# Another replay order for a hand-scheduled attention and MLP kernel: 1449 operations in a new sequence, 113 of them on another engine

## The chip, the core and the metric

The kernel runs on one core of a Trainium2 chip. A core has a matrix engine (TensorE, PE in the profile), a vector engine (VectorE, DVE), an activation engine (ScalarE, ACT), a general engine (GpSimd, POOL) and a sequencer that only issues transfers (SyncE, SP). Each engine takes its instructions strictly in the order in which the program lists them, and the engines meet through semaphores. The metric is the device time of one execution in microseconds (us); the figure of a kernel is the median of several runs.

## The reference

Two stages follow one another: a linear attention with cosine and sine weights, and a two-layer MLP with the gate `h * cos(h)`.

```python
# q, k, v: (8, 8, 576, 64) float32
r = maximum(x, 0); phi(x) = concat([r * cos(theta), r * sin(theta)], -1)   # theta by position
kv  = einsum('bhsf,bhsd->bhfd', phi(k), v);  z = sum(phi(k), axis=2)
num = einsum('bhsf,bhfd->bhsd', phi(q), kv); den = einsum('bhsf,bhf->bhs', phi(q), z) + 1e-6
x   = (num / den) as (4608, 512)
h   = x @ w_in                       # w_in (512, 2048)
out = (h * cos(h)) @ w_out           # w_out (2048, 512), out (4608, 512) float32
```

## The kernel before

The work is cut by batch. For a batch b of the eight, the attention loads q, k and v through SP, makes the features (`feat`, lines 240 and 242: a ReLU times a cosine or sine column, ten pieces of 128x512 for q and ten for k), casts v (`val`, line 222), multiplies k features with v on PE (`kv_half`, line 278), copies the result out (`kvz`), transposes the q features, multiplies them with kvz (`num_half`, line 287), divides (`den_add` and `ratio`, lines 295 to 307) and transposes the quotient into `xT`. For batches 0 and 1 the transposes of q and x, and for batch 2 those of x, run on PE (line 337); the later ones are DMA transposes that SP issues (lines 343 and 736). Four token tiles of a batch are one group of the MLP; the fifth tiles of all batches form one more group, `r`. The groups go in the order 0 to 6, `r`, 7.

The MLP's first layer (`moe1`, line 353, and `quad`, line 414 for groups 6, `r` and 7) multiplies xT with w_in into one of four PSUM slots called `m1`; ACT takes the cosine of it (`sin`, line 420), DVE or sometimes POOL multiplies both (`gate`, line 366) into `g`, and the gate frees the slot. The second layer (`prod`, line 469) uses a Strassen-Winograd form with seven products instead of eight for 2x2 blocks; it needs sums of blocks of g (`sums`, written to `s` and `g`), of w_out (`weight_sum`, WT), of w_in (`w_in_sum`, WS) and of x (`x_sum`, xs), all of them through line 366 on DVE or POOL. `z_add` and `y_add` of that form are DVE operations between a product and the next product into the same PSUM bank.

Nothing of the order is left to a scheduler. The functions `attention`, `layer1`, `quads` and `layer2` only register operations in a list, each with its number, the engines that could run it and its dependencies. `Plan.run` then walks through a text of 1449 entries, `ORDER`, and emits the operations in just that sequence:

```python
for x in ORDER.split():
    name, _, ids = x.partition(":")
    o, ids = self.ops[int(name.rstrip("VAG"))], [int(i) for i in ids.split(",") if i]
```

An entry such as `546:1` is operation 546 with buffer slot 1 of the ring it takes from; a letter behind the number picks the engine where there is a choice: V is DVE, A is ACT, G is POOL. Operations without a letter are PE's matmul groups, SP's and POOL's DMA issues, or bookkeeping. Since every engine runs its own instructions in this order, an entry that waits holds back all later entries of its engine, and a PE entry that waits holds back all of PE. The slot numbers matter too: `m1` has 4 slots, `qp`, `qT` 4, `ch` 3, `kvz` 3, `g` 2, and a slot's new user waits for its last one.

Entries that the text below speaks of, by number:

- 29, 30, 27: k features of batch 0 (DVE, DVE, ACT). 63 and 65: the two halves of its k-v product. 58, 60: transposes of its q tiles 3 and 4. 13 and 62: matmuls on zeros ("dummy").
- 247, 249: transposes of q tiles 2 and 3 of batch 1. 164, 160: first-layer tiles 6 and 5 of group 0, second half; 147, 159, 163, 167: the gates of tiles 1, 4, 5, 6. 213, 216, 228: features of batch 1. 253, 255: its k-v products; 254: the copy of the first one. 257: its first numerator.
- 303 to 312: the sums of w_out. 319, 320: the late sums of group 0. 360, 367, 369: k features of batch 2. 395: its k-v product.
- 422, 424, 427, 429, 432, 434: loads of q, k, v of batch 3 (two each). 393: DMA transpose of q tile 4 of batch 2. 437, 439, 441, 445, 446: k features of batch 3; 457, 461: two casts of its v; 969: a store of group 1; 472: the k-v product of batch 3. 443, 910, 919: a k feature of batch 3 and two gates of group 2.
- 488, 493: DMA transposes of x tiles 2 and 3 of batch 3. 546: DMA transpose of q tile 1 of batch 4. 492: the quotient that 493 reads; 532: a q feature that 546 reads. 983: the first matmul group on xT of batch 3.
- 1306, 1358: a gate of group 6, a `z_add` of group `r`. 1463, 1465, 1474, 1475: two `x_sum` and a `z_add` of group 7, and the matmul group that needs 1474.

Of the kernel before, what the change touches and what calls it, by code (L numbers as in the profile page):

```python
# [54 lines left out]
14 172:0 176:1 884:2 17:0 107:0 819:1 16:0 183:1 182:1 343:2 13 32V:0 34V:1 33A 35V 36A:2 52:0  # L55
54:1 53V:0 37A 38V:3 55A:1 56:2 40V:0 4G 24V 28A 5G 25V 62:3 31A 23V 7G 44A 30V 9G 39A 22V 41V
57A:2 42G 26V 45G 58:0 48V 51G 43A 60:1 46V 49G 27A 47V 29V 11G 61A:0 50V 63:0 59V:3 65:1 64V
66A 180 67:0 68V 77:1 69V:0 78A 72:0 79V:1 70:3 73A 71A 74V 87:1 80:2 88A 81A 89V:2 82:0 112:1
83A 84V 90:0 97:1 91V 102:0 98A 85:3 103A 108:2 99V:1 86A 184 75:0 76A 100:3 104V 92:1 93A 113
186 101A 94V 116:0 114A:0 189 109 115V 120:3 110A:1 191 117 111V 194 121 118A:2 136:1 122A:0  # L60
119V 95:2 196 137 96A 123V 128:0 138A:1 199 129 139V 124:2 130A:2 201 132:3 131V 133 105:1
134A:0 125 106V 148:0 126A:1 135V 144:1 223A:1 127V 149 140:3 150A:2 224G 225V:2 152:2 227V:3
226A 153 151V 141 154A:0 145 228V 142A:1 243:0 204G 155V 214A 205G 143V 245:2 244A:0 207G 215V
156:3 221V 146A:2 160:0 209G 213V 161 218A 147V 157 211G 220A 233V 164:1 237G 229V:0 158A:0 165
219G 216V 239A 159V 217A 230V 247:3 222A 235V 240G 231A:1 238V 234V 236V 246A:1 232G 173V 248A:3
253:2 174V 302V 166A:1 345 313:0 304V 254A 347 241A 167V 303G 242A 350 162A:2 257:3 255:2 352
258V 259V:0 249:1 256A 341 163V 262:3 250A:2 272:2 305G 321:1 263V 273V 264V 267:0 277:1 268V
265:3 278A 269V:2 266A 355 314 274V 306G 270:3 279V:1 315A:0 275:0 282:2 271A 316 357 276A 283A
280:1 284V 317 308G 281V 285:3 318A 287:0 286V 292:2 168:1 288V 293A 289V:2 260:3 370A:2 324:0
261V 294V 371A 307G 290:0 888:0 251:3 291V 372A:3 385:0 295:2 252V:1 169 296A 824:0 344:0 170A:0  # L70
825 820:3 826A:1 171V 374G:0 848:2 361A 827V 836:1 297 366A 319V 832:0 420:1 502:0 373A 175V
362G 821 833 822A:2 387:1 177V 849 834A:0 837 823V 850A:1 325 835V 380G 381A 856:3 309V 382G
384A 844:0 178V 375G 326A:1 845 857 846A:2 851V 322 838A:0 847V 852:2 383A 941:1 839V 179G 389:3
828:0 298A 364A 853 323V 840:1 854A:1 327V 829 365A 841 299V:1 328 320G 830A:2 855V 842A:0 331
368A 831V 300:2 329 301A 843V 360G 376A:1 310V 868:0 864:2 378A:2 332 330V 377A 367G 860:1 311V
858A:1 391:2 336 333A 861 859V 363A 337 334G 312V 862A:2 949:0 892:0 338A 369G 379V 865 863V 422
869 866A:0 880:3 424 870A:1 867V 881 339G 427 872:1 871V 882A:2 876:2 429 883V 877 393:1 873
885V 878A:0 395 421:1 874A:1 879V 396 875V 959:0 397A 418 889V 398 950 399A 886V 400V:0 960
951A:1 447A:3 957 890V 432 961A:2 449G:0 887V 952 945:2 891V 403 401:3 404A 958 405V:2 402A 434
448G 450A 953 1025:0 962V 451A:1 406:2 955V 408 452A 963 407V 462:0 439G 446A 409V 966 410V:1  # L80
453A:2 464:1 964 956V 954A 437G 454A 411:1 965V 413 967 412A 414V 415V:0 466:3 438A 971 441G
968V 416:3 468:2 457A 972 417V 460A 440V 917:2 976:1 443V 458A 969G 973V 455A:3 893:1 442V
918A:2 461G 920:0 444V 894A:0 919V 445G 899:3 921A:1 895V 456A 923:2 922V 900A:2 470:0 896:1
974G 924A:0 901V 459A 905:0 504 925V 897A:1 506 472 906A:2 898V 509 908:3 907V 511 473 909A:0
935:2 474A 500 910V 514 475 936A:1 929:1 476V 477V:2 926:0 930A:2 937V 478 480 927A:0 931V 911:3
481A 928V 902:2 912A:1 516 482V:1 914:1 903A:2 529G:0 913V 932:0 915A:0 483 904V 1033:0 933A:1
916V 530G 531A:1 934V 1034 533A:2 942V 485 938:3 1035A:1 486V 487V:0 532G 544:0 524A 1036 503:0
939A:2 943V 490 488 534A 491V 1041 940V 521G 528A 492V:2 546:1 1037 520A 525V 1038A 495 493 946V
579:1 661:2 542A 541G 1043:0 496A 947V 535G:3 540A 548:3 1044 1029:1 948V 539A 1042 519A 1040V
523A 1109:2 543G 527V 983:2 944V 536A 998:1 1039V 537A:0 550:2 986:0 497V:1 522A 538G 526A 995:3  # L90
1045V:0 498 999A:0 554 1046V 996A:1 552:0 555 1000V 984A:2 1047 577 997V 556A 581 985V 987A:0
557 992:1 583 558A 988V 586 1001:3 993A:1 559V:0 588 977:2 1002A:2 994V 560 562 978A:0 1003V
989:0 563A 979V 591 980:1 990A:1 564V:2 1010:3 981A:2 991V 567 593 1011A:0 1013:2 982V 606A:1
568V 1026G 1004:0 569V:1 1014A:1 565 1048 1005A:2 1012V 607A 572 1049V 570 1007:1 608G:2 573A
1006V 1050 1008A:0 1027V 621:0 596A 1051 1028V 602A 609G 1019:3 610V:3 1052A 574V:0 1055 1020A:2
612A:0 575 1021V 1016:0 1053G 1009V 613A 1117:0 623:1 1015V 617G 1017A:2 1056 620A 600V 611G
601V 616A 1118 1060:0 1057V 603A 1022:3 1018V 604A 619G 625:3 614V:1 1073:1 580:1 1023A:0 605G
1119A:1 1024V 1079:2 627:2 1074A:1 1030V 1120 597A 1075V 1058G 1082:0 618A 1031V 599A 1067:3
598G 1032V 1083A:2 1076:1 1068A:0 1084V 615A 1121 1069V 1077A:1 629:1 1064:0 1124V 1122A 1078V
1123G 1061:3 1065A:2 663 1080A:0 1066V 1125 665 1062A:1 1081V 668 1070:1 1063V 670 631 1071A:2  # L100
673 632 1072V 1127:0 633A 659 1110V 675 634 1113:0 1111V 1094:0 635A 636V:2 1126 1095A:0 637
1096V 639 1085:2 640A 688G:2 641V:1 1128 1086A:1 1112V 642 644 1129A:1 1193:1 1100:3 1087V
690G:3 689A 1130V 1088:1 645A 703:0 1101A:2 646V:0 1131 685A 680G 1102V 684A 649 1132 678V 683A
691V 1103:0 647 681A 1133V 679G 1097:2 1104A:0 687V 705:1 650V 1089A:1 1105V 1139 699A 1090V
1091:3 1098A:2 692G:0 651V:2 700A 1134 698A 1099V 652 654 702A 1135 738:1 694G:1 693V 1092A:0
707:3 1140 1136V 682A 1093V 701A 1201:0 1144:1 1137G 696A:2 1141V 1160:0 695V 697A 1142G 1154:1
709:2 1161A:1 1202 1155A:2 1162V 686G 740 655A 1156V 1151:2 1203A:1 742 656V:1 1148:3 1152A:0
1153V 1145:0 657 1149A:1 1150V 1157:1 1146A:2 711:1 1147V 1106:2 1158A:0 1159V 1204 1107A:1
662:0 1108V 713 745 1114V 1205 747 1115V 714 1206A 750 1209 1116V 715A 736 752 765A:3 1208V 716
1210 767V:0 1163:3 769V:1 768A 1207V 770G 771A:2 1211:0 766V 1164A:2 717V 1212 1197:2 780:0  # L110
718V:0 772A 1169:0 1310:0 1213A:2 1165V 719 1166:1 1170A:0 1214V 755G 757A 1171V 721 1172:2
782:1 1167A:1 722V 723V:2 756A 1178:3 763G 1173A:2 760V 1215 724 1168V 759A 726 1174V 1184:0
727A 784:3 776A 1194G 728V:1 1179A:0 1175:1 1185A:1 1180V 729 1181:2 1176A:2 1186V 731 1182A:0
775G 1216 786:2 1195V 777A 779G 1183V 1218 773A:3 1196G 1177V 764A 1219 732V 733V:0 762A 1187:3
1220A 1217V 734 1190:0 778G 1188A:1 758V 1221G 761A 1318:0 739:1 1189V 1191A:0 1223 1242V 774A
790 788:0 1192V 1319 1229V 1224 1230V 1232V 1233:2 1225A 1228:0 1198V 1234:1 1320A:1 1226G 791
1236V:0 1235A:3 1321 1231G 792A 1238 1253:0 1239A:2 1199G 1326 1240V 1237 793 1241V 1322 794A
795V:2 1200G 1243 1323A 1247 1244V 796 798 1248A:1 1254:2 799V 1245A:0 1250 1249V 1327 1251A:2
1324G 800V:1 1255A:1 1328:0 1252V 1256A:1 801 1257 1314:1 1258 1261V 1246G 1329 1259A:1 1260V
1262 1330A:2 1426:2 1325G 1266 1263V 803 1267A:2 1272:3 1331V 804A 1269 1264A:0 1268V 1332  # L120
1270A:1 805V:0 1265G 1273:0 1333 1275A:0 1271V 806 1311G 1274A:2 808 1334V 1335 809A 810V:2 1277
1276 1278A:2 811 813 1280V 1312G 1291:1 814A 815V:1 1281 1285 1282V 1336 816 1286A:0 1287V
1283A:1 1288 1340 1337A 1284G 1279V 1289A:0 1292:0 1290V 1434:0 1338G 1293A:3 1313V 1294A:1 1296
1295 1297A:2 1341 1299V 1298V 1300 1342A 1345:1 818 1301V 1343G 1435 1302A:1 1307 1436V:1 1304
1308A:0 1346G 1350:2 1305A:2 1309V 1437 1348G 1306V 1351:1 1438 1353A:2 1347V 1352A:3 1303V 1442
1439A 1440V 1369:0 1355 1349V 1354 1315G 1356A:0 1370 1358V 1444:0 1371A 1357V 1372A:0 1359
1430:0 1388:2 1360V 1373 1316V 1361A:2 1366 1363 1367A:1 1441V 1443 1364A:0 1368V 1362G 1445
# [925 lines left out]
```

## Time and profile before

| what | value |
|---|---|
| runs | 300.44, 298.2, 298.97, 299.27, 299.67 us |
| median | 299.27 us |
| the profiled execution, its own time | 300.44 us |
| its span, first to last instruction | 298.7 us |
| mean granted TensorE clock | 0.979 |
| PE matmul busy | 278.0 us (93%) |
| DVE busy | 239.8 us (80%) |
| ACT busy | 196.8 us (66%) |
| POOL busy | 187.9 us (63%) |

The profiled execution is the slowest of the five: its own time is 1.17 us above the median, and 1.74 us of it lie outside the span. Busy is the time in which the engine had an instruction under way; matmuls overlap, so a busy PE is not a PE at its full rate. An idle stretch in brackets in the timeline is the time the engine stood still before an instruction, with what released it.

### The profile page before, as it was taken

Reading aid. Unit: us, or ns where it says so; the run is one execution under the profiler, and the core shown is the slowest. Engines: PE = TensorE matmul, PEld = TensorE weight load, DVE = VectorE, ACT = ScalarE, POOL = GpSimd, SP = SyncE. Lnnn points to the kernel's source line nnn. Section 1 sums busy time; section 2 is a strip of 40 time slices with the busy share of each in tenths; the row PEclk is TensorE's granted clock in tenths of the full one; section 3 lists DMA queues with packets and bytes.
Section 4 is the critical chain, followed back from the end, with each engine's and each line's share of the span. In section 5 each row is a group of like instructions: output and inputs, shape, how many; then the busy total and the mean of one; then the engine's idle time right before and its main releaser. Section 6 shows DMA issues by size and latency. Waiting matters only on the chain.

```text
span 298.7 us, 7104 instructions
## 1 busy us (share of the span) xinstructions
PE 278.0 (93%) x2759; PEld 221.7 (74%) x2759; DVE 239.8 (80%) x430; ACT 196.8 (66%) x369; POOL 187.9 (63%) x169
## 2 busy tenths in 40 slices
PE   8869958999999999799999989999999999999992
PEld 8758846988897557457567747679998888878881
DVE  1876898799788899788979869995887998998860
ACT  2845896788566877768875956894656565746611
POOL 1510787999978639519956963784994634385900
PEclk9966999999999999999999999999999999999998
DMA  6999899934799999899959999995323102000203
GB/s 214 297 206 270 266 185 304 287 45 55 254 239 266 242 358 200 169 316 272 241 147 357 152 231 309 267 162 160 37 38 118 44 1 108 35 2 0 108 35 140
DMA packets 77248, 53.31 MB, mean 179 GB/s; under 512 B 46112, under 2 KB 74784, under 8 KB 77216
## 3 DMA queue, kind: packets, MB, share of 16 engines
q1 hardware_dynamic: 69920, 39.86, 56.7%
q0 software_dynamic: 6848, 12.59, 16.7%
q8 instruction: 21, 0.34, 0.5%
q10 hardware_dynamic: 448, 0.44, 0.4%
q14 instruction: 11, 0.09, 0.1%
HBM read 36.74 MB, written 9.44 MB: 155 GB/s over the span
## 4 chain that ended last, share of the span: by engine, by line
PE 55%; DMA 12%; DVE 11%; POOL 11%; ACT 4%; issue 3%; SPq 2%; ACTq 0%; DVEq 0%; POOLq 0%
PE M L353 16%; PE SD L469 10%; PE PZ L469 7%; DMA vm<-in_v_dram 6%; PE PX L469 6%; PE M L414 6%; PE SD L414 5%; POOL kp L242 3%; DMA km<-in_k_dram 3%; POOL WT L366 3%; PE KV L278 3%; DMA xT<-x 3%; DVE g L366 3%; DVE kp L242 2%; PE N L287 2%
## 5 line engine op out<-in xcount | busy, mean ns | idle before, releaser
L353 PE MATMUL M<-xT,w_in_sb 128*128 128x256 f16 (+1 forms) x512 | 92.6, 330 | 4.7 <-DMA xT<-x 2.2
L420 ACT ACTIVATE ch<-M 128x512 f32<-128x512 f32 x120 | 69.5, 595 | 37.0 <-PE M L353 22.8
L366 DVE TENSOR_TENSOR g<-M,ch 128x512 f16<-128x512 f32 x112 | 74.6, 685 | 19.1 <-ACT ch L420 18.0
L353 PEld LDWEIGHTS <-w_in_sb 128*128 128x128 f16 x512 | 49.3, 99 | 33.4 <-issue 3.6
L469 PEld LDWEIGHTS <-g 128*128 128x128 f16 x640 | 61.5, 98 | 11.1 <-POOL g L366 0.5
L242 POOL TENSOR_SCALAR qp<-qm,CS 128x512 f16<-128x512 f32 x19 | 41.4, 2183 | 27.9 <-DMA qm<-in_q_dram 27.9
L242 POOL TENSOR_SCALAR kp<-km,CS 128x512 f16<-128x512 f32 x17 | 37.2, 2196 | 6.6 <-DMA km<-in_k_dram 4.1
L469 PE MATMUL PX<-w_out_sb,g 128*128 128x256 f16 x256 | 32.9, 272 | 0.0
L240 ACT ACTIVATE qp<-qm,CS 128x512 f16<-128x512 f32 x41 | 27.9, 714 | 6.4 <-DMA qm<-in_q_dram 4.7
L307 DVE TENSOR_TENSOR x<-N,rec 128x512 f16<-128x512 f32 (+1 forms) x44 | 26.2, 594 | 3.0
L240 ACT ACTIVATE kp<-km,CS 128x512 f16<-128x512 f32 x40 | 27.3, 716 | 1.3 <-DMA km<-in_k_dram 1.3
L469 PEld LDWEIGHTS <-s 128*128 128x128 f16 x256 | 24.5, 98 | 4.7 <-issue 0.6
L414 PEld LDWEIGHTS <-w_in_sb 128*128 128x128 f16 x192 | 18.5, 98 | 3.9 <-issue 0.9
L366 POOL TENSOR_TENSOR s<-g 128x512 f16<-128x512 f16 x10 | 11.9, 1210 | 10.5 <-DVE den L297 9.9
L469 PE MATMUL PZ<-w_out_sb,g 128*128 128x256 f16 x128 | 16.4, 273 | 0.3 <-POOL g L366 0.3
L469 PE MATMUL PZ<-WT,s 128*128 128x256 f16 x128 | 16.3, 273 | 0.2 <-ACT ost L220 0.2
L242 DVE TENSOR_SCALAR kp<-km,CS 128x512 f16<-128x512 f32 x23 | 16.1, 731 | 0.4 <-DMA km<-in_k_dram 0.4
L278 PE MATMUL KV<-V,kp 128*128 128x65 f16 x320 | 13.5, 199 | 2.7 <-DVE kp L242 1.3
L287 PE MATMUL N<-kvz,qT 128*128 128x65 f16 x256 | 15.0, 200 | 0.9 <-DVE x L307 0.3
L287 PEld LDWEIGHTS <-qT 128*128 128x128 f16 x256 | 13.0, 102 | 3.7 <-DVE x L307 1.5
L278 PEld LDWEIGHTS <-kp 128*128 128x128 f16 x320 | 12.4, 101 | 4.4 <-DVE kp L242 1.4
L242 DVE TENSOR_SCALAR qp<-qm,CS 128x512 f16<-128x512 f32 x20 | 11.1, 575 | 5.4 <-DMA qm<-in_q_dram 5.4
(137 smaller groups left out, 501.5 us busy)
## 6 DMA issues: line engine op xcount, KB each, us to landing
out_dram<-ost POOLq DMA_DIRECT2D x28, 256.0 KB, 3.0
qm<-in_q_dram SPq DMA_DIRECT2D x8, 640.0 KB, 5.5
km<-in_k_dram SPq DMA_DIRECT2D x8, 640.0 KB, 7.5
qm<-in_q_dram SPq DMA_DIRECT2D x8, 512.0 KB, 6.5
km<-in_k_dram SPq DMA_DIRECT2D x8, 512.0 KB, 8.6
vm<-in_v_dram SPq DMA_DIRECT2D x6, 640.0 KB, 9.2
vm<-in_v_dram SPq DMA_DIRECT2D x6, 512.0 KB, 8.7
w_in_sb<-in_moe_w_in_dram POOLq DMA_DIRECT2D x4, 512.0 KB, 8.4
```

Of the source, the lines that this page charges most:

```text
L240: nc.scalar.activation(out=dst, in_=src, func=AF.Relu, scale=sc)
L242: (nc.vector if eng == "V" else nc.gpsimd).tensor_scalar(out=dst, in0=src, scalar1=0.0, scalar2=sc, op0=ALU.max, op1=ALU.mult)
L278: nc.tensor.matmul(tile_[:, n, hh, :], lhsT=kps[b][:, t, h].rearrange("p g d -> p (g d)"), rhs=V1[:, t, h, :], start=(t == 0), stop=(t == NT))
L287: nc.tensor.matmul(tile_[:, n, hh, :], lhsT=qT(p, t)[:, h, :], rhs=kvzs[p][:, h, :], start=(i == 0), stop=(i == len(parts) - 1))
L307: nc.vector.tensor_tensor(out=dst, in0=tile_[:, :, :, 0:D], in1=rec.unsqueeze(3).broadcast_to((P, nb, HB, D)), op=ALU.mult)
L353: nc.tensor.matmul(ps[key][:, n, :], lhsT=w_in_sb[:, c, j * P:(j + 1) * P], rhs=x[:, c, s0:s1], start=(c == 0 and n == 0), stop=(c == NCT ...
L366: (nc.vector if eng == "V" else nc.gpsimd).tensor_tensor(out=out, in0=in0, in1=in1, op=op)
L414: nc.tensor.matmul(ps[(g, qd, bank)][:, i, :], lhsT=lhs[:, c, 2 * qd + i, :], rhs=rhs[:, c, :], start=(first and i == 0 and c == 0), stop= ...
L420: nc.scalar.activation(out=ps[("ch", key)], in_=ps[key].rearrange("p j s -> p (j s)"), func=AF.Sin, bias=math.pi / 2.0, scale=1.0)
L469: nc.tensor.matmul(ps[(g, bank)][:, i, :], lhsT=lhs[:, j, i * P:(i + 1) * P], rhs=rhs[:, c * HJ // 2 + j], start=(first and i == 0 and j = ...
```

## The change

Only the text `ORDER` is replaced. The same 1449 operations are emitted; 587 of them have no engine letter in either text and keep their engine, 749 keep their letter, and 113 change it: 24 from ACT to DVE, 21 from DVE to ACT, 23 from POOL to ACT, 21 from ACT to POOL, 16 from DVE to POOL, 8 from POOL to DVE. An entry moves by 6.4 places on average, at most by 91, and 256 entries take another buffer slot. The number of instructions of each kind, their shapes and their dependencies stay as they were, except where a DVE sum of 128x1024 becomes two POOL sums of 128x512.

The diff, cut to the entries that this text speaks of:

```diff
-14 172:0 176:1 884:2 17:0 107:0 819:1 16:0 183:1 182:1 343:2 13 32V:0 34V:1 33A 35V 36A:2 52:0
-54:1 53V:0 37A 38V:3 55A:1 56:2 40V:0 4G 24V 28A 5G 25V 62:3 31A 23V 7G 44A 30V 9G 39A 22V 41V
-57A:2 42G 26V 45G 58:0 48V 51G 43A 60:1 46V 49G 27A 47V 29V 11G 61A:0 50V 63:0 59V:3 65:1 64V
+14 107:0 819:1 172:0 176:1 884:2 16:0 182:1 343:2 17:0 183:1 13 32A:0 33V 34A:1 52:0 35V 36A:2
+53V:0 54:1 38A:3 37V 40A:0 39V 56:2 4G 29V 24A 58:3 5G 41V 55A:1 22V 7G 60:0 46V 26A 28V 62:1 9G
+23V 57A:2 44G 42V 43G 31V 51A 45G 48V 50A 25V 47G 27A 11G 30V 61V:0 49A 63:0 59A:3 65:1 64V 67:0
...
-156:3 221V 146A:2 160:0 209G 213V 161 218A 147V 157 211G 220A 233V 164:1 237G 229V:0 158A:0 165
-219G 216V 239A 159V 217A 230V 247:3 222A 235V 240G 231A:1 238V 234V 236V 246A:1 232G 173V 248A:3
-253:2 174V 302V 166A:1 345 313:0 304V 254A 347 241A 167V 303G 242A 350 162A:2 257:3 255:2 352
+150A:2 221V 209G 164:1 146A:0 151V 165 211G 222A 228V 160:2 233G 147V 217A 161 219G 237V 247:0
+214A 238V 235V 220A 216V 213V 246A:1 234G 236V 230V 231A:1 253:3 173V 166A:1 232G 174V 240A
...
-858A:1 391:2 336 333A 861 859V 363A 337 334G 312V 862A:2 949:0 892:0 338A 369G 379V 865 863V 422
-869 866A:0 880:3 424 870A:1 867V 881 339G 427 872:1 871V 882A:2 876:2 429 883V 877 393:1 873
+422 870A:1 337 863V 424 878A:2 880:3 871V 393:1 892:0 338A 872:0 360A 879V 339G 881 873 885V
+882A:0 427 395 421:1 874A:1 883V 396 875V 950 429 397A 418 889V 398 951A:1 959:1 432 886V 399A
...
-939A:2 943V 490 488 534A 491V 1041 940V 521G 528A 492V:2 546:1 1037 520A 525V 1038A 495 493 946V
+939A:0 490 488 535A:3 491V 1041 940V 520A 519G 492V:1 1037 523A 532V 495 493 1038A 1039V 579:1
+661:2 539A 1043:0 540G 946V 546:1 543A 536G 1029:1 947V 1044 542A 548:3 528A 527V 1042 944V
...
-1425V 1558 1468A:0 1422V 1469A:1 1554 1431V 1471 1555A 1556V 1485:1 1472A:1 1560:0 1463V 1465V
-1470 1546:2 1473V 1432G 1561 1474V 1486 1562A:2 1475 1487V 1488A:0 1479 1433G 1476V 1490 1480A:2
+1467:1 1425V 1558 1468A:3 1431V 1469A:1 1554 1464V 1471 1556V 1555A 1485:2 1472A:0 1463V 1560:1
+1432G 1473V 1470 1546:2 1486 1474V 1561 1487A 1488V:2 1489 1562A:0 1465V 1479 1493V 1557G 1490
+1480A:2 1475 1491A:1 1481V 1559 1476V 1498 1433G 1563V 1477A:0 1482 1504:0 1499A:2 1492V 1564
```

## The prediction

> **What bounds the kernel now.** I read the page first (busy times, the clock row), then busy time by stage, then who waits for whom in the stages where PE is not full, and last the timeline of the one engine that PE waits for there.
>
> ```profile
> span 298.7 us, 7104 instructions
> PE 278.0 (93%) x2759; PEld 221.7 (74%) x2759; DVE 239.8 (80%) x430; ACT 196.8 (66%) x369; POOL 187.9 (63%) x169
> ...
> PEclk9966999999999999999999999999999999999998
> ```
>
> PE's row and columns say that it is the bound: the same matmuls run in any order, so only PE's idle time can change. By stage (start:end, then length, then busy time of PE, PEld, DVE, ACT, POOL, clock):
>
> ```profile
> 16.50:18.00 1.50, 1.13 (x21) 1.13 (x22) 1.12 (x3) 0.00 (x0) 0.00 (x0) 0.56 1.25 207
> ...
> 25.50:27.00 1.50, 1.50 (x8) 1.04 (x8) 0.60 (x2) 0.90 (x3) 0.00 (x0) 0.53 1.01 357
> ...
> 40.00:50.00 10.00, 6.20 (x93) 5.08 (x93) 9.66 (x23) 7.71 (x14) 6.91 (x6) 1.00 1.18 235
> 50.00:75.00 25.00, 24.50 (x263) 21.75 (x261) 22.09 (x44) 20.12 (x41) 25.00 (x18) 1.00 0.66 150
> ...
> 100.00:125.00 25.00, 22.69 (x211) 14.61 (x210) 22.09 (x39) 18.73 (x34) 15.80 (x11) 1.00 1.11 250
> ```
>
> Three things are to be seen. From 16.5 to 27 us the clock (third column from the right) is near a half. From 40 to 50 us DVE is full and PE idles 3.8 us. Later PE is nearly full, and what is left are single holes: 1.69 us at 120, 1.11 at 173, 0.55 at 145, 0.59 at 264 and some of 0.3. POOL is full from 50 to 75. The holes and the work behind them are in the timeline (start, length, engine; in brackets PE's idle time before the group and what ended it). The long one at 120 and the queue that it waits for, SP's:
>
> ```profile
> 121.56 1.47 PE L353 MATMUL M<-xT,w_in_sb 128*128 128x512 f16 x6 [1.69 <-DMA xT<-x]
> ```
> ```profile
> 115.35 2.07 SPq L736 DMA_TRANSPOSE xT<-x  x1
> 117.60 1.23 SPq L343 DMA_TRANSPOSE qT<-qp  x1
> 118.93 1.23 SPq L736 DMA_TRANSPOSE xT<-x  x1
> ```
>
> The holes at 42 and 264, both ended by DVE, and DVE's work before the second:
>
> ```profile
> 43.05 0.61 PE L337 MATMUL TP<-IDENT,qp 128*128 128x128 f16 x8 [1.51 <-DVE g L366]
> ...
> 264.57 0.60 PE L414 MATMUL SD<-xT,w_in_sb 128*128 128x256 f16 x4 [0.59 <-DVE M L366]
> ```
> ```profile
> 260.64 2.67 DVE L366 TENSOR_TENSOR xs<-xT,xs 128x512 f16<-128x512 f16 x2
> ```
>
> POOL's k features of 70 to 81 us, and SP's loads and a transpose just after:
>
> ```profile
> 72.07 5.09 POOL L242 TENSOR_SCALAR kp<-km,CS 128x512 f16<-128x512 f32 x2
> ...
> 78.34 2.00 POOL L242 TENSOR_SCALAR kp<-km,CS 128x512 f16<-128x512 f32 x1
> ```
> ```profile
> 80.37 0.60 SPq L232 DMA_DIRECT2D km<-in_k_dram  x1
> 81.75 4.49 SPq L343 DMA_TRANSPOSE qR<-qp  x1
> ```
>
> **The change part by part.** I compare the two orders at each hole: what stands before the late producer on its engine, priced by its rows.
>
> *Start.* The k-v product 63 begins in earnest at 16.87, behind DVE's feature 29 (ends 16.82). In the new order 29 runs early; the last features are 30 on DVE and 27 on ACT. After v's last part lands (15.1) DVE does a cast, 25 and 30: 0.6 + 0.5 + 0.5, so 16.4 us. Gain 0.4.
>
> *40 to 50 us.* Transpose 247 waits for gate 159 (its slot's last user), which ends at 42.99. In the new order 247 takes another slot, freed by gate 147, and DVE reaches 147 without 213 (0.82), 216 (0.83), a cast (0.58) and one q feature, but with another q feature: 2.2 us less, so 40.8 instead of 43.0. The idle 0.92 + 1.51 us shrinks to about 0.3. But 213 and 216 then stand between 247 and product 253, so 253's last input comes at about 43.5 instead of 44.5: 1.0 gained. Two waits are new: copy 254 stands behind two casts and a cosine on ACT (45.7, as now), and 257 and 255 take slots freed by gates 167 and 163, which DVE reaches at 47.3 and 48.0; 255 starts at 46.07 now, and PE is held behind both. Adding on, the same amount of PE work (30.7 us of it) is done at 49.7 against 50.3, and after the next ratios (quotients on DVE) 0.3 to 0.9 is left. For the start and this stage together I take 0.5; bounds -0.5 and 1.3.
>
> *70 to 81 us.* POOL runs 46.5 to 81.4 without a hole and ends late with 320 (72.08, PE waits 0.42) and 369 (80.34, PE waits 0.49 at product 395). The new order takes a w_out sum (2.26), feature 360 (2.95), 369 (2.00) and a cast (1.08) off POOL, and puts sum 319 (2.3) and a cast (0.64) on it: 5.4 us less. The two features cost ACT 2 x 0.72 in a stage where it is busy 20.1 of 25. Both holes go, 0.9. I take 0.7, since at 427 the k loads of batch 3 may come later: 393 now stands in front of them and a transpose behind loads takes up to 4.49 us on SP. They would then be issued at 81.2 against 80.37; v's loads come at 82.5 instead of 86.3. On POOL only 441, 446, 457, 969, 437 (7.9 us) then stand between k's landing (90.9 now) and product 472, where 439, 437, 441, 969, 461, 445 took 9.85.
>
> *98 us.* A matmul group waits 0.3 us for gate 919 behind four features. The new order's gate 910 has 443 behind it, 0.8 earlier. Gain 0.3.
>
> *120 us.* 983 waits for transpose 493, issued at 118.93, landed at 121.5, 2.6 us later. Its input 492 was done at 115.94; it waited only for SP, where 546 (1.23) stands in front of it. In the new order 546 comes behind, so 493 goes out at 117.5 and lands at 120.1; PE arrives at 119.87. Gain 1.3 to 1.5, taken 1.3. 546's input 532 goes to DVE (0.58) from POOL (2.0) and is ready before; 546 moves from 117.60 to about 118.8 and the transposes behind it end at the same time.
>
> *145 and 173 us.* The transposes there have the same SP issues ahead of them. No gain.
>
> *238 us.* `z_add` 1358 ends at 238.04 at the end of a full DVE run from 231.95. Gate 1306 (0.6) leaves that run for an earlier place. The hole is 0.33; gain 0.3.
>
> *264 us.* `x_sum` 1465 (1.25) moves behind `z_add` 1474, and 1475 moves three matmul groups (1.3) back. The hole of 0.59 goes; gain 0.6.
>
> Sum of named gains: 0.5 + 0.7 + 0.3 + 1.3 + 0.3 + 0.6 = 3.7.
>
> *What the moves cost.* Net by engine, pieces times their rows: DVE -4.1 us, ACT +0.6, POOL +11.7; until 140 us of PE work POOL is 3 to 5 us lighter, later up to 12 heavier, mostly by five sums (2.3 each, two instructions) and a gate (1.3 against 0.69). Each has over 2 us to its first user now, except sum 1317, which then ends near 243 for a product at 245.7. POOL is busy 83.3 of the last 138.7 us (busy time by stage, 160:298.7), so 55.4 idle us hide this; without them the 11.7 would show.
>
> A rule that speaks against it: the trace has DVE's k features from 0.469 to 1.20 us (mean 0.731), the longer ones beside a busy POOL, while gates, which read PSUM and SBUF, stay at 0.673 to 0.692. [...] By the nominal rows DVE gains 4.1. All excess over the shortest of each kind is about 16 us for 188 us of POOL, 0.087 per us, so 11.7 more cost 1.0: DVE still gains 3.1. I take the trace's rate.
>
> *New holes.* Each old hole is a wait that an order met on the chip; the new one will meet its own. Nothing in the trace shows them. From below they cost 0; from above, as much as the named gains, 3.7. PE's idle time, summed over the stages from 50 to 275 us, is 6.1, about 0.27 per 10 us; with 3.2 of that removed over the places I followed, I take half back: 1.5.
>
> Forecast: -3.7 + 1.5 = -2.2, so 298.2 for the profiled execution (300.44). It is 1.17 above the median of 299.27, and the same difference from the median gives 297.1; I say 297.0.
>
> **The rivals.**
>
> *The clock stays up* (0.20). It fell at 16.7 and came back at 26.9; the product's idle stretch is 14.9 to 16.87. [...] In the new order 58 and 60 run before the dummies 62, these then fill 12.4 to 14.9, and the gap is 1.4. [...] At half clock the 4.3 us of full-rate work between 16.9 and 26.9 take 8.6, and DVE's quotients take most of the rest: at most 3, I say 1.5 more, 295.5. Against: the loads of batch 1 land when they land.
>
> *New holes eat it* (0.22): they cost the upper bound, and the time is 299.0 to 299.3.
>
> *Slower: the k loads of batch 3* (0.16). If 393 is held on SP, they land later than 90.9. POOL's shorter list and PE's head start allow until about 91.5; each us beyond that is a us of PE at 472. To be slower by 0.5% they must land after 95.2, two long transposes late: 301.0. For it: the 4.49 above. Against: v's loads come earlier.
>
> That the order does not reach the chip is excluded: each engine's list of instructions differs.
>
> **How the numbers follow.** Forecast 0.42 (295.8 to 298.3). A measurement of this kernel can tell about 0.5%, 1.5 us, from no change: faster means below 297.8. Of the forecast three quarters lie there and all of the clock case: 0.52. The rest of the forecast and the eaten case: 0.30. The k loads and a remainder of the eaten case: 0.18. Range 294.6 to 300.5: it takes in the clock case and the eaten one and leaves out the slow one.
>
> **What would show it.** Right: no hole before the first matmul on xT of batch 3 (493 issued straight after 488); no POOL wait before product 395; the hole before 247 below 0.5 with one of about 1.5 before 257; `z_add` before 1475 without wait; DVE near 237 busy, POOL near 199. Wrong: a hole over 1 us at any place not named, PE busy plus holes unchanged, or k of batch 3 landing after 92. The clock row in the fourth slice tells the clock case.

## The result, and the profile after

The changed kernel takes 297.27 us (median of 43 runs, 294.71 to 300.06), before 299.19 us (80 runs): ratio 0.9946, 95% interval 0.9929 to 0.9962. Here and below medians hold all executions, while ratios leave out those over 1.5% above the fastest of their kernel, so the two need not agree. The forecast was 297.0. The profiled execution of the changed kernel took 296.81 us with a span of 295.0; that of before took 300.44 with 298.7. The two executions are 3.6 us apart and the medians 1.9, so a good part of what the two traces show side by side is chance of the two executions. How much, and where, had to be found with further runs.

The page after; first the span and the engines' busy times, then the granted clock in 40 slices:

```profile
span 295.0 us, 7115 instructions
...
PE 275.1 (93%) x2759; PEld 219.9 (75%) x2759; DVE 238.5 (81%) x425; ACT 196.0 (66%) x368; POOL 197.1 (67%) x179
...
PEclk9999979999999999999999999999999999999999
```

PE's 278.0 us have become 275.1, with the same 2759 matmuls: the clock now stays up at the start (1.00 from 15 to 41 us) and, while PE works, is low in one stretch only, at 0.50 from 41.1 to 44.5 us. DVE fell by 1.3 us where I had forecast about 3 (near 237), POOL rose by 9.2 (197.1, forecast near 199). The same stages as before, with 41 to 44 and 125 to 150 us as well (start:end, length, busy time of PE, PEld, DVE, ACT, POOL, clock, DMA share, GB/s):

```profile
16.50:18.00 1.50, 1.13 (x38) 1.05 (x36) 1.34 (x3) 0.10 (x1) 0.17 (x1) 1.00 1.23 203
25.50:27.00 1.50, 1.50 (x16) 1.35 (x14) 1.04 (x3) 0.98 (x2) 0.00 (x0) 1.00 1.05 371
41.00:44.00 3.00, 2.35 (x28) 1.69 (x25) 2.84 (x5) 2.62 (x7) 1.83 (x2) 0.52 1.24 207
40.00:50.00 10.00, 7.60 (x107) 6.21 (x108) 8.42 (x24) 6.31 (x16) 8.83 (x8) 0.83 1.18 256
50.00:75.00 25.00, 25.00 (x255) 22.55 (x254) 21.72 (x40) 21.15 (x40) 22.70 (x17) 1.00 0.72 163
100.00:125.00 25.00, 23.99 (x223) 14.88 (x220) 21.98 (x41) 19.71 (x37) 14.06 (x8) 1.00 1.06 229
125.00:150.00 25.00, 23.37 (x168) 14.58 (x167) 21.57 (x34) 18.57 (x35) 19.87 (x17) 1.00 1.04 254
```

From 50 to 75 us PE has no idle time left and POOL is no longer full. From 100 to 125 PE gained 1.3 us of busy time; from 125 to 150 it lost 1.1 (24.45 before). The holes in PE's timeline of the changed kernel:

```profile
40.82 1.06 PE L278 MATMUL KV<-V,kp 128*128 128x65 f16 x20 [1.93 <-ACT ch L420]
...
42.95 1.44 PE L469 MATMUL PX<-w_out_sb,g 128*128 128x256 f16 x6 [0.65 <-DMA w_out_sb<-in_moe_w_out_dram]
...
117.03 3.63 PE L353 MATMUL M<-xT,w_in_sb 128*128 128x512 f16 x16 [0.59 <-DMA xT<-x]
...
142.05 2.75 PE L353 MATMUL M<-xT,w_in_sb 128*128 128x512 f16 x12 [1.25 <-ACT SD L220]
...
170.51 1.02 PE L353 MATMUL M<-xT,w_in_sb 128*128 128x512 f16 x4 [1.18 <-DMA xT<-x]
...
259.44 0.60 PE L414 MATMUL SD<-xs,WS 128*128 128x256 f16 x4 [0.69 <-DVE xs L366]
```

The hole at 120 is down from 1.69 to 0.59 us and the one before 1475 is gone. The one of 0.55 at 145, before tile 1070, has become 1.25 (now at 142), and the one before product 253 has become 1.93 (0.68 before). New are 0.69 before group 1470, 0.39 for a gate at 140.08, and a wait for the load of w_out (0.65) that the trace before did not have.

To compare executions I use PE's progress. The names in the first column are those of the experiments below. From each trace I take the time at which PE has done the same amount of matmul work, counting every matmul at its duration without a wait at full clock (for example 0.218 us for 512 columns; in the profile of before eight of 256 columns took 0.87 us, from 81.66). The difference to the profile of before is PE's lead, in us. Columns are the us of work done; extra dummy matmuls are not counted as work. first_820, which lost 7 us at the place where its two orders join, is left out.

| execution | lead at 50 | at 90 | at 110 | at 125 | at 160 | at 220 | at the end |
|---|---|---|---|---|---|---|---|
| changed kernel | 2.16 | 3.53 | 4.54 | 3.29 | 3.21 | 3.32 | 3.48 |
| changed_again | 1.80 | 3.17 | 4.81 | 4.11 | 4.83 | 4.44 | 4.60 |
| start_only | 0.88 | 1.38 | 2.22 | 2.34 | 2.97 | 2.96 | 2.96 |
| rest_only | 0.53 | 1.90 | 3.24 | 2.38 | 2.89 | 2.95 | 3.09 |
| swap_546 | 0.16 | 0.31 | 1.82 | 1.26 | 0.91 | -0.62 | -0.62 |
| dummy_more | -0.65 | -0.07 | 0.07 | -0.08 | 0.51 | -0.57 | -0.58 |
| no_dummy | 0.09 | 1.47 | 2.86 | 2.87 | 4.13 | 4.19 | 4.35 |
| sp_575 | 0.01 | 1.39 | 2.83 | 3.25 | 3.08 | 3.18 | 3.33 |
| x_first | -0.10 | 1.28 | 2.82 | 2.46 | 3.13 | -0.86 | -0.12 |
| first_821 | -0.36 | 1.02 | 2.78 | 2.21 | 2.09 | 2.09 | 2.09 |
| sp_xsum | 1.94 | 3.32 | 5.06 | 5.46 | 5.84 | 5.91 | 6.65 |
| sp_xsum_dummy | 0.85 | 2.22 | 3.80 | 3.81 | 4.45 | 4.51 | 5.25 |

Two things stand out. From 50 to 90 us of work every run with the changed order there gains 1.37 or 1.38 us on the profile of before. But that profile is only one of its order: the three other traces that have the order of before in this stretch gain on it too, 0.15 (swap_546), 0.50 (start_only) and 0.58 us (dummy_more). So the order is worth 0.8 to 1.4 us here, 1.1 against the mean of the four. Up to 50 the runs with the changed order from the first entry spread from 0.36 behind to 2.16 ahead: that is not the order.

### The profile page after: what moved, and what is told of

Read it like the earlier page. It is cut to its first block, busy times and chain, and to the rows that moved or that the text cites. A ratio compares the mean times of both kernels' runs of the same rounds, so it can differ in the third digit from the quotient of the medians.

```text
span 295.0 us, 7115 instructions
## 1 busy us (share of the span) xinstructions
PE 275.1 (93%) x2759; PEld 219.9 (75%) x2759; DVE 238.5 (81%) x425; ACT 196.0 (66%) x368; POOL 197.1 (67%) x179
## 4 chain that ended last, share of the span: by engine, by line
PE 67%; DMA 15%; DVE 11%; issue 2%; SPq 1%; POOL 1%; ACT 1%; DVEq 0%; POOLq 0%; ACTq 0%
PE M L353 21%; PE SD L469 11%; PE PZ L469 8%; PE PX L469 8%; PE M L414 6%; DMA km<-in_k_dram 5%; PE SD L414 5%; DMA w_out_sb<-in_moe_w_out_dram 4%; PE KV L278 3%; DMA vm<-in_v_dram 3%; DMA xT<-x 2%; PE N L287 2%; DVE g L366 2%; DVE qp L242 2%; PE PY L469 1%
## 5 line engine op out<-in xcount | busy, mean ns | idle before, releaser
L353 PE MATMUL M<-xT,w_in_sb 128*128 128x256 f16 (+1 forms) x512 | 90.6, 326 | 3.7 <-DMA xT<-x 1.8
L242 POOL TENSOR_SCALAR qp<-qm,CS 128x512 f16<-128x512 f32 x21 | 46.1, 2201 | 28.1 <-DMA qm<-in_q_dram 11.0
L469 PE MATMUL PX<-w_out_sb,g 128*128 128x256 f16 x256 | 34.5, 277 | 1.4 <-DMA w_out_sb<-in_moe_w_out_dram 1.0
L242 POOL TENSOR_SCALAR kp<-km,CS 128x512 f16<-128x512 f32 x15 | 32.4, 2166 | 1.9 <-DMA km<-in_k_dram 1.6
L240 ACT ACTIVATE kp<-km,CS 128x512 f16<-128x512 f32 x44 | 30.0, 715 | 3.0 <-DMA km<-in_k_dram 2.5
L240 ACT ACTIVATE qp<-qm,CS 128x512 f16<-128x512 f32 x38 | 25.9, 714 | 5.6 <-DMA qm<-in_q_dram 5.6
L242 DVE TENSOR_SCALAR qp<-qm,CS 128x512 f16<-128x512 f32 x21 | 15.1, 742 | 5.8 <-DMA qm<-in_q_dram 5.8
L504 POOL DMA_DIRECT2D out_dram<-ost x14 | 8.3, 591 | 12.0 <-ACT ost L220 11.9
L414 PEld LDWEIGHTS <-WS 128*128 128x128 f16 x144 | 13.9, 98 | 2.7 <-issue 0.9
L220 ACT ACTIVATE V<-vm 128x512 f16<-128x512 f32 (+1 forms) x26 | 13.9, 570 | 1.7 <-DMA vm<-in_v_dram 1.7
```

The source lines that it names most:

```text
L220: nc.scalar.activation(out=out, in_=in_, func=AF.Copy)
L240: nc.scalar.activation(out=dst, in_=src, func=AF.Relu, scale=sc)
L242: (nc.vector if eng == "V" else nc.gpsimd).tensor_scalar(out=dst, in0=src, scalar1=0.0, scalar2=sc, op0=ALU.max, op1=ALU.mult)
L353: nc.tensor.matmul(ps[key][:, n, :], lhsT=w_in_sb[:, c, j * P:(j + 1) * P], rhs=x[:, c, s0:s1], start=(c == 0 and n == 0), stop=(c == NCT ...
L414: nc.tensor.matmul(ps[(g, qd, bank)][:, i, :], lhsT=lhs[:, c, 2 * qd + i, :], rhs=rhs[:, c, :], start=(first and i == 0 and c == 0), stop= ...
L469: nc.tensor.matmul(ps[(g, bank)][:, i, :], lhsT=lhs[:, j, i * P:(i + 1) * P], rhs=rhs[:, c * HJ // 2 + j], start=(first and i == 0 and j = ...
```

## The experiments

In the kernels other than changed_again line numbers are one to five higher, because the text of the order has other line breaks or code was added. Entries not named so far: 313 and 314 are the first two products with w_out; 332 and 923 are matmul groups that waited for POOL and for a gate. 575 is the last DMA transpose of x of batch 4, and 1070 the first-layer tile that needs it; 621 is a transpose of q of batch 5; 647 and 652 are transposes of x of batch 5, and 1160 the tile that needs them; 703 to 709 are transposes of q of batch 6. 1470 is the matmul group that needs `x_sum` 1463, and 1556 a y sum on DVE.

**start_only and rest_only: where does the gain sit?** Both orders hold the same set of entries in their first 61, so they can be joined there.

```diff
-ORDER = before
+ORDER = changed[:61] + before[61:]      # start_only
+ORDER = before[:61] + changed[61:]      # rest_only
```

> The first 61 entries (up to the copy behind the k-v product of batch 0) in the changed order, everything after them in the order of before. Clock theory (the gain of the start is TensorE's clock, which no longer falls behind the k-v product, because the dummies run later): granted clock full from 12 to 30 us, first-layer tile 112 or 108 done about 2.5 us sooner than before, and at the end 1 to 2.5 us less than before (ratio 0.992 to 0.997). Hole theory (the gain lies in the named holes from 40 us on): ratio 0.999 to 1.001 even where the clock stays up, because the stage of 40 to 50 us is set by DVE and waits there for the same features.

> The complement: the first 61 entries as before, the rest in the changed order. Clock theory: granted clock near a half from about 17 to 27 us as before; the holes at 72, 80, 98 and 120 us are gone all the same, but most of the gain is not: 0 to 1 us less than before (ratio 0.997 to 1.000). Hole theory: 1.5 to 2.5 us less than before (ratio 0.992 to 0.995), the whole of the change.

Measured: start_only 0.9895 (0.9844 to 0.9947, 6 runs), rest_only 0.9945 (0.9915 to 0.9976, 12 runs). The medians are 297.17 us for both, against 299.39 for before beside them. rest_only has the clock near a half from 17 to 24 us (0.55 on average from 17 to 20, 0.59 from 20 to 25) and still the whole gain: the hole theory. start_only has the full clock there (1.00) and cannot be read as the rival half: its trace leads by 0.88 at 50, and 2.1 of its 2.96 at the end came later, under the order of before. So the profile of before lost time that its order does not demand, which fits its 300.44 against a median of 299.19. Each half alone measures as much as the whole change, so the two do not add up, and what the start's order is worth on its own stays open within these intervals.

**dummy_more and no_dummy: what is the clock at the start worth?** One adds dummies to before where PE idled, the other takes those of entry 62 out of the changed order.

```diff
 60:1
+1609:3        # dummy_more: dummies("m1", 30)
...
-62:1          # no_dummy
```

> The order of before with one entry more: 30 matmuls on zeros (about 1.8 us at full clock) straight behind transpose 60, so that TensorE is busy from 14.9 to about 16.7 us, where it idled. No other entry moves. Clock theory: the granted clock does not fall at 16.7 us, and PE's work of the next 10 us is done up to 2.5 us sooner; time 1 to 2.5 us less than before (ratio 0.992 to 0.997), like the run with the changed start. If it was not the idle stretch that lowered the clock, the clock falls as before and the time is the same (0.999 to 1.001).

> The changed order without the 45 dummy matmuls 62. TensorE then idles from about 12.7 to 15.2 us. If the start's granted clock sets the end: the clock falls at about 13 or 17 us for two or three windows, and the time is 1 to 2.5 us more than the changed kernel (ratio to before 0.998 to 1.003). If it does not (as the run with more dummies has it, where the clock stayed up and the time did not fall), the clock falls likewise and the time is within 0.5 us of the changed kernel (ratio 0.993 to 0.997).

The windows 13:17, 17:27 and 38:41 us, first of dummy_more, then of no_dummy:

```profile
13.00:17.00 4.00, 3.08 (x51) 2.79 (x52) 3.50 (x9) 3.27 (x5) 3.40 (x7) 1.00 1.08 168
17.00:27.00 10.00, 8.54 (x123) 7.05 (x124) 7.83 (x24) 5.63 (x18) 0.41 (x3) 1.00 1.05 185
...
38.00:41.00 3.00, 0.96 (x12) 0.66 (x10) 3.00 (x6) 3.00 (x6) 3.00 (x4) 1.00 1.08 159
```
```profile
13.00:17.00 4.00, 0.55 (x5) 0.32 (x6) 4.00 (x8) 3.62 (x7) 3.69 (x7) 0.77 1.02 163
17.00:27.00 10.00, 9.11 (x102) 7.45 (x103) 6.50 (x23) 3.96 (x13) 0.42 (x3) 0.58 1.13 209
...
38.00:41.00 3.00, 2.08 (x21) 1.46 (x18) 3.00 (x6) 3.00 (x6) 3.00 (x3) 1.00 0.98 146
```

The clock does what was aimed at, up in one (1.00 from 17 to 27 us) and down in the other (0.58). In no_dummy it was low for some 10 us (worked out from the 0.77 and 0.58, taking 0.50 for low), about as long as in the profile of before, where it was 0.50 from 16.7 to 26.9 us. That is three of the expectation's windows, if one is the changed kernel's stretch of 3.4 us from 41.1 to 44.5. The time does not follow: dummy_more 1.0015 (0.9988 to 1.0042), which leaves room for a gain of 0.4 us at most, no_dummy 0.9954 (0.9917 to 0.9990), close to the changed kernel's own ratio. The third lines show why. With the clock up PE arrives early at 38 us and finds little to do: it is busy 0.96 of 3 us, and 0.80 in the changed kernel, whose order no_dummy shares and which with the clock down is busy 2.08. The lead turns into a wait for product 253 and for what follows it, and behind that wait the clock falls after all: in dummy_more it is 0.50 from 43.6 to 50.4 us. The chain of waits of dummy_more's trace runs through the load of k of batch 1, until 34.3 us, and that of w_out, until 51.2, not through PE.

**changed_again: how much of the first profile was chance?** The same kernel once more.

> The changed kernel once more, for a second profile of it. In its first profile PE stood 2.15 us ahead of before at 50 us of its work; in three runs with the same order up to there it stood 0.0 to 0.4 ahead. If that first profile was the exception: 0 to 0.8 ahead at 50 us of work, a wait of 2 us or more before product 253 with a low clock behind it, and 1.4 us gained from 50 to 90 us of work as in every run with this order. If the order itself gives it: about 2 us ahead again.

Measured: 0.9894 (0.9846 to 0.9943, 6 runs), lead 1.80 at 50 and 1.37 more by 90. So the good start came twice, while three of the other runs with the same entries up to there (sp_575, x_first, first_821) have not got it. What goes with it is when k of batch 1 is in. POOL issues the four loads of w_out only behind a small cast that waits for k, here in the changed kernel and in x_first:

```profile
32.86 0.54 POOL L533 CAST w_out_sb<-km 1x1 f16<-1x1 f32 x4 [1.05 <-DMA km<-in_k_dram]
33.42 3.27 POOL L547 DMA_DIRECT2D w_out_sb<-in_moe_w_out_dram  x4
```
```profile
34.30 0.54 POOL L534 CAST w_out_sb<-km 1x1 f16<-1x1 f32 x4 [1.97 <-DMA km<-in_k_dram]
34.87 3.27 POOL L548 DMA_DIRECT2D w_out_sb<-in_moe_w_out_dram  x4
```

and PE in x_first, where product 313 then waits for that load:

```profile
44.52 1.44 PE L470 MATMUL PX<-w_out_sb,g 128*128 128x256 f16 x6 [1.49 <-DMA w_out_sb<-in_moe_w_out_dram]
```

The cast starts at 32.40 (changed_again), 32.85 (sp_xsum) and 32.86 us (changed kernel) in the three executions that lead by 1.8 to 2.2 at 50, and at 33.61 (sp_575), 33.86 (first_821) and 34.30 (x_first) in those that lead by nothing. The link is not one to one: start_only leads by 0.88 with its cast at 34.14, first_820 by 0.37 with its at 33.09. The wait of product 313 for w_out is 0.65 us in the changed kernel and 1.49 in x_first. The chain of waits of the changed kernel runs through this too: by its own shares of the span, first of before, then of the changed kernel,

```profile
PE M L353 16%; PE SD L469 10%; PE PZ L469 7%; DMA vm<-in_v_dram 6%; PE PX L469 6%; PE M L414 6%; PE SD L414 5%; POOL kp L242 3%; DMA km<-in_k_dram 3%; POOL WT L366 3%; PE KV L278 3%; DMA xT<-x 3%; DVE g L366 3%; DVE kp L242 2%; PE N L287 2%
```
```profile
PE M L353 21%; PE SD L469 11%; PE PZ L469 8%; PE PX L469 8%; PE M L414 6%; DMA km<-in_k_dram 5%; PE SD L414 5%; DMA w_out_sb<-in_moe_w_out_dram 4%; PE KV L278 3%; DMA vm<-in_v_dram 3%; DMA xT<-x 2%; PE N L287 2%; DVE g L366 2%; DVE qp L242 2%; PE PY L469 1%
```

w_out's load (4%) is on the chain only after. In the traces of the changed kernel, dummy_more and x_first the end of this stage is so set by loads, one behind another, and not by PE's speed before it. That k comes in at another time from run to run is measured; why, is not.

**swap_546: the step at 120 us alone.**

```diff
-492V:... 546:1 ... 493
+492V:... 493 546:1
```

> The order of before with one pair exchanged on SP's queue: transpose 493 (x of batch 3) ahead of transpose 546 (q of batch 4). Step of the prediction: the hole of 1.69 us before tile 983 shrinks to 0.2 to 0.4, 1.3 us gained there, and kept: ratio 0.995 to 0.997. Rival (given back): the transposes of x of batch 4 are issued when they were, paced by the ratios and SP's own queue, so the hole before tile 1073 at 145 us grows from 0.55 us by about what was gained, 1 to 1.3, and the end is within 0.3 us of before (0.999 to 1.001).

Measured: 0.9948 (0.9910 to 0.9987, 12 runs). The hole:

```profile
119.75 3.63 PE L354 MATMUL M<-xT,w_in_sb 128*128 128x512 f16 x16 [0.78 <-DMA xT<-x]
```

From 1.69 to 0.78 us, less than expected, and PE's lead rises by 1.5 from 90 to 110 us of work. In the same trace the hole at 145 us is 1.11 us, where it was 0.55, half of what the rival asks, and a new one of 1.19 follows at 151; the lead is gone by 130 us of work. But this execution took 301.10 us against its kernel's median of 298.47. The times say that a gain is kept, of 0.4 to 2.7 us by the interval: the 1.3 of the prediction fits, and they show no more than that.

**sp_575: SP's queue at 142 us.**

```diff
-621:0 ... 575
+575 621:0
```

> The changed order with one entry moved on SP's queue: transpose 621 (q of batch 5, not needed before about 152 us) behind transpose 575 (x of batch 4). Theory (SP's queue holds 575: its ratio is done at 135.8 us, it goes out at 136.9, behind 621): 575 goes out within 0.3 us of its ratio, the wait before tile 1070 falls from 1.64 us to 0.5 or less. Then two ways: kept to the end, ratio to before 0.990 to 0.992; or given back at the next transposes of x, with the hole before tile 1160 at 170 us growing from 1.2 to 2 us or more, ratio 0.993 to 0.996 as the changed kernel itself.

Measured: 0.9897 (0.9847 to 0.9946, 6 runs); the interval reaches the changed kernel's 0.9946, so the times do not tell kept from given back. 575 went out 0.03 us behind its ratio, and tile 1070 lost 0.26 us instead of 1.40. That alone would not prove it, since PE came there 1.7 us later than in the changed kernel's profile. The fair pair is changed_again and sp_xsum, with leads of 4.81 and 5.06 ahead of this place: transpose 575 goes out at 135.85 and 135.03 us, and tile 1070 loses 1.37 and 0.27:

```profile
141.23 2.75 PE L353 MATMUL M<-xT,w_in_sb 128*128 128x512 f16 x12 [1.22 <-ACT SD L220]
```
```profile
139.88 2.75 PE L354 MATMUL M<-xT,w_in_sb 128*128 128x512 f16 x12
```

In all ten traces that have the changed order here, 1070 starts 0.09 us after 575 has landed (in the changed kernel issued at 136.92, landed 5.0 us later, start at 142.05), so it is the transpose that it waits for, though the profile names ACT's copy for SD (its PSUM slot had been free since 140.03 in the changed kernel). Of the 1.35 us by which the tile starts sooner in sp_xsum, 0.82 is the earlier issue; the rest is a shorter way from issue to landing, 4.8 us against 5.3, which the edit does not explain.

**x_first: all transposes of x first.**

```diff
-544:0 ... 493            703:0 647 ... 705:1 ... 652
+493 544:0                647 ... 652 703:0 705:1
-621:0 ... 575            1556V ... 1463V
+575 621:0                1463V 1556V
```

> The changed order with all the transposes of q that stand just ahead of a late transpose of x put behind it (544 behind 493, 621 behind 575, 703 and 705 behind 652) and with x_sum 1463 ahead of the y sum 1556 on DVE. Theory: the holes before tiles 983 (0.6), 1070 (1.6) and 1160 (1.2) shrink to 0.3 or less each and the one of 0.7 before 1470 goes, so 2.5 to 3.5 us less than the changed kernel, ratio to before 0.983 to 0.987. Rival (the landing of the transposes is set by the transfers themselves, not by SP's order): the holes keep their sum of about 3.4 us, ratio 0.993 to 0.996.

Measured: 1.0020 (0.9989 to 1.0051). A miss, and neither theory had it. The holes at 983 and 1160 fell below 0.2 us, the one at 1070 to 0.57, and 4.1 us of lead were lost at 189: a wait of 2.5, and behind it the clock, which was 0.73 on average from 190 to 193 us. PE, then DVE:

```profile
188.65 1.87 PE L470 MATMUL SD<-w_out_sb,g 128*128 128x256 f16 x8 [2.54 <-DVE PZ L367]
```
```profile
183.76 0.48 DVE L243 TENSOR_SCALAR qp<-qm,CS 128x512 f16<-128x512 f32 x1 [2.08 <-DMA qm<-in_q_dram]
...
186.68 0.48 DVE L243 TENSOR_SCALAR qp<-qm,CS 128x512 f16<-128x512 f32 x1 [1.60 <-DMA qR<-qp]
187.08 0.68 DVE L223 COPY p<-PZ 128x512 f32<-128x512 f32 x1
187.90 0.70 DVE L367 TENSOR_TENSOR PZ<-SD,p 128x512 f32<-128x512 f32 x1
```

Behind the moved pair, SP issues 707 and 709 and then batch 7's q load, now at 175.63 us instead of 171.00. DVE's q features wait for that load and for a slot that the transpose into qR frees, and behind them in DVE's order stands the `y_add` that product 1215 needs. The moved transposes had some 15 us of slack (the first numerator of batch 6 is at 182 us); the loads behind them on the same queue had none.

**first_820 and first_821: the end of the order.** Both orders hold the same set in their first 821 entries.

```diff
+ORDER = changed[:821] + before[821:]     # first_821: slots of m1, x16, ch renamed behind the joint
```

> The changed order for the first 821 entries (up to the ratio of batch 5's first tile, about 155 us), the order of before from there. Prediction's steps at 238 and 264 us: they are worth 0.9 us, so this run loses them and is 0.9 us above the changed kernel (ratio to before 0.996 to 0.999). Rival (the wait at 264 only moved from product 1475 to 1470, and the one at 238 stayed): the time is that of the changed kernel, ratio 0.992 to 0.996.

> As the run with the changed order for the first 821 entries and the order of before behind them, with the slot numbers behind the joint renamed so that no slot is taken again by the very next user (the earlier run lost 6.3 us at the joint, where ratio 641 waited for the transpose that had just begun to read its slot). Prediction's steps at 238 and 264 us: 0.9 us above the changed kernel (ratio to before 0.995 to 0.999). Rival (the wait at 264 only moved from 1475 to 1470, and the one at 238 stayed): ratio 0.992 to 0.995.

first_820 measured 1.0199 (1.0133 to 1.0264), by the place where the two orders join. DVE's timeline:

```profile
157.01 0.20 DVE L304 RECIPROCAL rec<-den 128x8 f32<-128x8 f32 x1
163.92 0.69 DVE L308 TENSOR_TENSOR x<-N,rec 128x512 f16<-128x512 f32 x1 [6.70 <-DMA xT<-x]
```

Ratios 636 and 641 had got the same x16 slot, and DVE stood still for 6.70 us until the transpose had read it: the price of one slot number. With the slots renamed, first_821 measures 0.9954 (0.9920 to 0.9988), just inside the first expectation, and too wide to tell it from the second. The trace does: from 220 us on its lead does not change, nor do those of start_only, dummy_more and swap_546 by more than 0.01, where the whole changed order gains 0.16. Two steps that I had put at 0.9 are worth 0.16.

**sp_xsum and sp_xsum_dummy: a better order?**

```diff
-621:0 ... 575       -1556V ... 1463V
+575 621:0           +1463V 1556V
+if b == 1 and hbs == (0,):              # sp_xsum_dummy only, ahead of product 253
+    for _ in range(54): matmul(KV, zero, zero[:, 0:65])
```

> The changed order with two entries moved: transpose 621 behind 575 on SP's queue, and x_sum 1463 ahead of the y sum 1556 on DVE. If both waits go as they went in the two runs before: 0.3 to 0.7 before tile 1070 where the changed kernel had 1.4, at most 0.3 before products 1470 and 1482 together where it had 0.9; 1 to 1.5 us less than the changed kernel, ratio to before 0.988 to 0.992. If PE's lead is given back at the next transposes of x: ratio 0.992 to 0.996.

> The same, and 54 matmuls on zeros of 65 columns (about 1.8 us) in front of the k-v product 253 of batch 1, into the bank that it then overwrites, so that TensorE is busy while it waits for 253's features. Theory (what is left of the wait at 40 us costs twice, by the wait and by the clock that falls behind it): granted clock full from 40 to 46 us, product 313 loses under 0.9 us where it lost 2.5 to 2.7, and 1 to 1.7 us less than the run without these dummies (ratio to before 0.983 to 0.989). Rival (DVE's features, sums and gates set the stage, and the clock only fills what would be a wait): full clock, but the wait turns up before 257, 249 or 321, and the time is within 0.5 us of the run without.

sp_xsum measures 0.9861 (0.9811 to 0.9912), median 295.34 us; the changed kernel beside it 0.9894 (0.9846 to 0.9943), 295.70. The intervals overlap and the medians are 0.36 us apart where 1 to 1.5 was expected, so that it is faster than the changed kernel is possible and not shown by the times; the trace shows the two waits gone. From 220 us to the end sp_xsum and x_first, both with 1463 moved, gain 0.74 where the changed order gains 0.16. sp_xsum_dummy has full clock throughout (1.0 on average), 0.9868 (0.9812 to 0.9923), 295.08 us: no difference that can be told from sp_xsum. Its trace loses 1.45 us before 257 and 1.85 before 314 instead. This is the rival, and the same answer as at the start: the clock alone is worth nothing that shows here.

## Why the prediction was right, step by step

The time is right (297.0 against 297.27) and most of the way there too; three terms of the sum were mis-sized. That the total comes this close is in part luck: the end of the order brought 0.7 us less than forecast, one wait grew where nothing was forecast, and the lump of 1.5 us that I had taken off for new holes covers both.

- **Start and 40 to 50 us, 0.5 taken, -0.5 to 1.3 as bounds.** The seven profiles with the changed order from the first entry and with its dummies (first_820 led by 0.37) lead by 0.83 on average at 50, from -0.36 to 2.16. The base of this average is one profile; swap_546, with the order of before up to here, leads it by 0.16. The size is right; the mechanism only in part. The start gained nothing in time: the last feature ends at 16.90 against 16.82. Transpose 247 came sooner as said, with a wait of 0.27 us. But the 1.5 us that I expected before 257 is 0.49, and 1.93 stands before 253, over 1 us at a place not named, one of my own signs of being wrong. I looked for the limit on DVE and ACT; the chain of waits runs through the loads of k and w_out.
- **70 to 98 us, 0.7 + 0.3.** 1.37 us against the profile of before, alike in all ten profiles that have this order (first_820 among them): 0.42 before 332, 0.49 before 395 and 0.45 before 923. That all of it is the order's doing is not shown. In start_only and dummy_more, with the order of before here, the waits before 332 and 395 are gone too, since POOL is through sooner, and the one before 923 costs 0.87 and 0.79 instead. POOL's feature 369 in start_only, which the profile of before has at 78.34:

```profile
75.48 2.00 POOL L244 TENSOR_SCALAR kp<-km,CS 128x512 f16<-128x512 f32 x1
```

Against the mean of the four profiles with the order of before the gain is 1.1, close to the 1.0 forecast. The 0.2 that I had kept back for the k loads was not needed: 393 took 1.31 us on SP, not 4.49, and the k load went out at 76.93 instead of 80.37. The slower rival did not come.
- **120 us, 1.3.** 1.01 in the first profile, 1.64 in the second, 1.76 at most (90 to 110 in the table). Right in size. 493 goes out behind 488 as said; the hole that was to vanish is still 0.59 us in the first profile and gone in the second.
- **145 us, "The transposes there have the same SP issues ahead of them. No gain."** The step that failed by its size. The same issues stand ahead, but PE now comes 4.5 us sooner and SP's queue only 3.2: the wait before 1070 grew from 0.55 to 1.25 us, so 0.70 was given back where nothing was forecast. It is 1.22 in changed_again and 0.52 in no_dummy, so this too differs between executions. Before, 575 went out 0.03 us after its ratio; after, it stands behind 621 until 136.92, with its ratio done at 135.79:

```profile
130.60 3.79 SPq L736 DMA_TRANSPOSE xT<-x  x2
134.49 2.34 SPq L343 DMA_TRANSPOSE qT<-qp  x1
136.92 1.97 SPq L736 DMA_TRANSPOSE xT<-x  x1
```

- **238 and 264 us, 0.3 + 0.6.** 0.16. At 238 the gate left its run as said, and `z_add` still came last. At 264 the wait went from 1475 to 1470, the second mis-sized step. DVE, then POOL:

```profile
255.52 0.68 DVE L366 TENSOR_TENSOR sr<-gr 128x1024 f16<-128x1024 f16 x1
256.12 0.42 DVE L366 TENSOR_TENSOR xT<-xT 128x512 f16<-128x512 f16 x1
256.45 1.64 DVE L366 TENSOR_TENSOR gr<-gr,sr 128x1024 f16<-128x1024 f16 x1
258.02 1.37 DVE L366 TENSOR_TENSOR xs<-xT,xs 128x512 f16<-128x512 f16 x1
```
```profile
256.36 2.75 POOL L366 TENSOR_TENSOR sr<-sr,gr 128x512 f16<-128x512 f16 x2 [2.54 <-DVE sr L366]
```

Beside POOL's sums DVE's y sum takes 1.64 us and x_sum 1463 takes 1.37, and the product behind them waits. I had looked at what moved behind 1474 and not at what then stood in front of 1463.
- **New holes, 1.5.** In the first profile the lead falls by 1.25 us from 110 to 125: 0.70 is the grown wait before 1070, the rest a product at 140.08 that waits 0.39 us for a gate. That gate stands behind two q features which DVE does beside POOL's sums:

```profile
135.71 3.71 DVE L242 TENSOR_SCALAR qp<-qm,CS 128x512 f16<-128x512 f32 x2
```

The lump is near that in size; it named neither place.
- **The clock case.** Its sign came true, the clock stayed up (1.00 from 15 to 20 us, 0.67 before); its 1.5 us did not. That a shorter idle stretch would keep it up was my estimate, and no run shows at which length the clock falls: in the changed kernel PE idled 0.93 and 0.37 us before the k-v product's matmuls at 16.32 and 16.95. PE's speed there is covered by the waits from 38 us on, as dummy_more and no_dummy show. Nor was the idle stretch before it one of 2 us: in the profile of before one matmul stands in it, at 15.35, and the longest idle part is 1.32 us.
- **DVE 3.1 us lighter by the trace's rate of 0.087 us per us of POOL.** It is 1.3. If the rest of the nominal 4.1 is excess beside POOL, which grew by 9.2, it is 0.3 us per us of POOL and not 0.087; that is an estimate from two single executions. Where it fell on a wait, at 258 us, it took back the step.

In the first profile the sum is 2.16 + 1.37 + 1.01 - 1.25 + 0.03 (125 to 220) + 0.16 = 3.48, against 2.2 forecast. What was too much in it is the start, which differs between executions, and some 0.3 us of the 1.37 that the profile of before lost by chance.

## What to carry to other kernels

A lead is worth something only as far as the next thing that does not move with it: here a chain of loads at 43 us and SP's queue at 137, so follow the late producer's queue with PE's new arrival time, not the old one. Where a step is moved on an in-order queue, look at the loads behind it before its own slack. Before a hole is charged to the order, take further profiles of both kernels: from 50 to 90 us the changed order came back within 0.02 us ten times, while the order of before, against which it was measured, spread over 0.58.

## What the runs showed of the hardware

One DVE feature of q, of a kind that took 0.47 us at 35.51 in the profile of before, took 2.99 in changed_again while POOL ran two tensor sums from 136.06 to 138.33. Lines of changed_again, DVE and POOL:

```profile
135.64 2.99 DVE L242 TENSOR_SCALAR qp<-qm,CS 128x512 f16<-128x512 f32 x1
```
```profile
136.06 2.27 POOL L366 TENSOR_TENSOR g<-g 128x512 f16<-128x512 f16 x2
```

It ended 0.3 us behind POOL's sums; the changed kernel's first profile has the same picture (two features in 3.71 us, above). The lines show the size, some six times the 0.47 us, beside two POOL sums in a row; by what mechanism, no trace here shows. Also, behind the idle stretch ahead of product 253 the clock was 0.50 from 42 to 44 us in the changed kernel (idle for 1.93 us) and in sp_xsum (1.58 us, with 0.30 more behind three matmuls), and 1.00 in changed_again (1.79 us): the length of one gap alone did not decide it.
